# Later loads spread over ten tiles, the next pair's preparation over four, its signs a tile later

## The chip, the cores and the metric

The kernel runs on one core of one Trainium2 chip. The metric is the device time of one execution in microseconds (us); for the kernel before and after it is the median of several runs. A core has TensorE (PE in the rows, its weight loads PEld), VectorE (DVE), ScalarE (ACT), GpSimd (POOL), SyncE (SP, which here only issues DMAs) and 16 DMA engines.

## The reference

Three stages follow one another, for 2 batches of 768 rows and a width of 512.

```python
# 1: attention in hash buckets, 8 heads of 64
q_bits = (einsum('bhsd,dk->bhsk', q, proj) > 0)      # 6 bits, the same for k
mask = q_bucket[:, :, :, None] == k_bucket[:, :, None, :]
scores = np.where(mask, scale * q @ k.T, -1e9)
attn_out = softmax(scores) @ v
# 2: mixing over the rows (rank 32) and an MLP of 2048
u = x + (x.T @ U @ V).T
x = u + np.maximum(u @ w_ch1, 0.0) @ w_ch2
# 3: four causal attention experts of width 64, the two best by a gate
out = sum over e of mask_e * w_e * (softmax(causal(scale * (x wq[e]) (x wk[e]).T)) @ (x wv[e]) @ wo[e])
```

## The kernel before

The scheduler of the language puts each engine's instructions in order at build time: every instruction has a priority, its place in the program (some places are shifted), and each engine's list is filled by priority as instructions become ready in a modelled time. What the program order says is therefore not always the order on an engine; SP's queue runs in the order so found, and a DMA that waits holds all behind it.

The first attention works in pairs of heads, 4 pairs in each of 2 batches. A pair has 12 tiles of 128 query rows, 6 for each head (`a1_head`). A tile has the score matmuls (L606 with AQ and AK, L611 with BQ and BK, into PSUM tile sc), DVE's minimum on the way out (L617), ACT's exponential (L526) and then one of two ways. In most tiles P is split into a high and a low half (L528 and L534) and a DMA transposes both (L628, PT<-HL), after which 18 matmuls (L538 to L540) give po. In half of the first batch's tiles the transpose is done by TensorE in float32 (L581) with 6 matmuls L590 of four passes each.

AQ, AK, BQ and BK hold the queries and keys of a pair, split into high and low float16 parts, with the hash bits as extra rows. They are made one pair ahead: `a1_stream` calls `ahead()` when a pair begins, which calls `a1_prep` for the next pair and `a1_load` for the one after it. `a1_prep` does the following at once, in program order: ACT and DVE make QN from qn (L403, L404), a DMA transposes it to AQ (L407); ACT and POOL make KN (L408, L409), transposed to AK (L412); POOL makes the low keys KL (L414), transposed to KT (L418); plain copies bring AQ into BQ (L419) and KT into BK (L421); `a1_values` makes V (L454 POOL, L455 ACT, L456 POOL). Then `signs()`, put off by `later(wait, signs)`, computes the hash bits on TensorE (L436), compares on DVE (SG, L441) and brings them into rows of BQ and BK by four copies (L446, L447). AQ, AK, BQ, BK and V have two buffers each, qn, kn, vn, QN, KN and KL one.

`later(n, fn)` runs fn after n more tiles, and `tick()` is called once a tile; entries due at the same tick run in the order in which they were put in. The wait of the signs is SIGN_LAG (L1124), 6. The loads of a pair (`a1_load`, six of 192 KB, in the order q, k, q, k, v, v) are put off by 1 to 6 tiles (L382 to L384). When the last pair is reached, `moe2_weights` runs SIGN_LAG + 1 tiles later and loads the weights of stage 3. For the very first pair `ahead` itself is put off by two tiles.

Beside the tiles run the MLP's weight loads (`w64_unit`, 32 of 512 KB, L278, which DVE, ACT and POOL turn into float16 halves, L189 to L195 and L281 to L283), one unit for each two tiles of the first batch. The mixing of a finished pair (`x_stage_a`, `b`, `c`) follows 1, 5 and 8 tiles into the next pair. From the second batch's third pair on, TensorE also gets the MLP's matmuls (L734, L754), merged in a fixed proportion.

Of the kernel before, what the change touches and what calls it, by code (L numbers as in the profile page):

```python
# [15 lines left out]
AF = mybir.ActivationFunctionType  # L16
ALU = mybir.AluOpType
# [5 lines left out]
def kernel(  # L23
# [17 lines left out]
    nc = tc.nc  # L41
    B, H, S, D = q.shape
# [30 lines left out]
    XP = (0, 40)  # L73
    XV = True
    LUV = 4
    PLAG = (0,150)
    VLAG = 150
    PJ = nc.vector
# [34 lines left out]
    def halves(n):  # L113
        return [(c, min(512, n - c)) for c in range(0, n, 512)]
# [16 lines left out]
        out=penU, in_=penU, pattern=[[1, P]], base=0, channel_multiplier=-1,  # L131
# [11 lines left out]
    for c, kinds in enumerate(((0, 0, 1, 1), (0, 1, 0, 1))):  # L143
        for i, kind in enumerate(kinds):
# [3 lines left out]
                out=thr[sl, c : c + 1], in_=thr[sl, c : c + 1], pattern=[[0, 1]],  # L148
# [196 lines left out]
    def later(n, fn):  # L345
        pending.append([n, fn])
# [10 lines left out]
    def sooner(n, fn):  # L357
        tc.cur_priority -= n
        fn()
        tc.cur_priority += n  # L360
# [7 lines left out]
    def a1_load(b, p, spread=True):  # L368
        h0 = 2 * p
        qn = sp.tile([P, 2 * NT, D], F32, tag="qn", name=f"qn_{b}_{p}")  # L370
        kn = sp.tile([P, 2 * NT, D], F32, tag="kn", name=f"kn_{b}_{p}")
        vn = sp.tile([P, 2 * NT, D], F32, tag="vn", name=f"vn_{b}_{p}")
        jt = [slice(NT * j, NT * (j + 1)) for j in range(2)]
        todo = []
        for j in range(2):
            todo.append((qn[:, jt[j], :], q[b, h0 + j].rearrange("(t p) d -> p t d", t=NT)))
            todo.append((kn[:, jt[j], :], k[b, h0 + j].rearrange("(p t) d -> p t d", t=NT)))
        for j in range(2):
            todo.append((vn[:, jt[j], :], v[b, h0 + j].rearrange("(p t) d -> p t d", t=NT)))
        nats[b, p] = (qn, kn, vn)  # L380
        todo = [lambda d=d, s_=s_: nc.sync.dma_start(d, s_) for d, s_ in todo]
        if spread:  # L382
            for i, fn in enumerate(todo):
                later(1 + i, fn)  # L384
        return todo

    preps = {}

    def a1_prep(b, p, wait):
        qn, kn, vn = nats.pop((b, p))  # L390
        n = f"{b}_{p}"
        QN = sp.tile([P, 2 * NT, P], FH, tag="QN", name=f"QN_{n}")
        KN = sp.tile([P, 2 * NT, P], FH, tag="KN", name=f"KN_{n}")
        KL = sp.tile([P, NT, P], FH, tag="KL", name=f"KL_{n}")
        AQ = sp.tile([P, 2, NT, P], FH, tag="AQ", bufs=2, name=f"AQ_{n}")
        AK = sp.tile([P, 2, NT, P], FH, tag="AK", bufs=2, name=f"AK_{n}")
        BQ = sp.tile([P, 2, NT, P], FH, tag="BQ", bufs=2, name=f"BQ_{n}")
        BK = sp.tile([P, 2, NT, P], FH, tag="BK", bufs=2, name=f"BK_{n}")
        KT = sp.tile([P, NT, P], FH, tag="KS", bufs=2, name=f"KT_{n}")
        V = sp.tile([P, 2, 2 * NT, D], FH, tag="V", bufs=2, name=f"V_{n}")  # L400
        flat = lambda ap: ap.rearrange("p j t s -> p (j t) s")
        jt = [slice(NT * j, NT * (j + 1)) for j in range(2)]
        nc.scalar.activation(QN[:, :, 0:D], qn, AF.Copy, scale=-0.125)  # L403
        nc.vector.scalar_tensor_tensor(  # L404
            QN[:, :, D : 2 * D], QN[:, :, 0:D], 8.0, qn, op0=ALU.mult, op1=ALU.add
        )
        nc.sync.dma_start_transpose(out=flat(AQ), in_=QN)  # L407
        nc.scalar.activation(KN[:, :, 0:D], kn, AF.Copy)  # L408
        nc.gpsimd.tensor_scalar(  # L409
            KN[:, :, D : 2 * D], KN[:, :, 0:D], -0.125, 1.0, op0=ALU.mult, op1=ALU.mult  # L410
        )
        nc.sync.dma_start_transpose(out=flat(AK), in_=KN)  # L412
        for j in range(2):
            nc.gpsimd.tensor_tensor(  # L414
                KL[:, :, D * j : D * (j + 1)], kn[:, jt[j], :], KN[:, jt[j], 0:D],
                op=ALU.subtract,
            )
        nc.sync.dma_start_transpose(out=KT, in_=KL)  # L418
        nc.sync.dma_start(BQ[0:D], AQ[0:D])  # L419
        for j in range(2):  # L420
            nc.sync.dma_start(BK[0:D, j], KT[D * j : D * (j + 1)])  # L421
        preps[b, p] = (AQ, AK, BQ, BK, V)
        a1_values(b, p, vn, V)

        def signs():
            sg = psc.tile([P, 1024], F32, tag="sc", name=f"sg_{n}")
            f2 = lambda ap: ap.rearrange("p t s -> p (t s)")
            for c0, cn in halves(S):
                cs = slice(c0, c0 + cn)

                for last, ops in enumerate((
                    ((PQ, AQ[:, 0]), (PQ, AQ[:, 1]), (PK, AK[:, 0]), (PK, AK[:, 1])),
                    ((PL, AQ[:, 0]), (PL, AQ[:, 1]), (PB[:, 0], KT), (PB[:, 1], KT)),
                )):
                    for i, (w, x) in enumerate(ops):
                        nc.tensor.matmul(  # L436
                            sg[32 * i : 32 * (i + 1), cs], w, f2(x)[:, cs],
                            start=(last == 0), stop=(last == 1), skip_group_check=True,
                        )
            SG = sp.tile([P, NT, P], FH, tag="KS", bufs=2, name=f"SG_{n}")  # L440
            nc.vector.tensor_scalar(  # L441
                f2(SG), sg[:, 0:S], thr[:, 0:1], far[:, 0:1], op0=ALU.is_lt, op1=ALU.mult
            )
            rows = slice(D, D + NR)
            for j in range(2):
                nc.sync.dma_start(BQ[rows, j], SG[32 * j : 32 * j + NR])  # L446
                nc.sync.dma_start(BK[rows, j], SG[64 + 32 * j : 64 + 32 * j + NR])  # L447

        later(wait, signs)

    def a1_values(b, p, vn, V):
        f32 = any(x[0] == "F" for x in A1_MODES[b][p])
        V32 = VF[p % 2] if f32 else vn
        nc.gpsimd.tensor_scalar(V32, vn, 16.0, 1.0, op0=ALU.mult, op1=ALU.mult)  # L454
        nc.scalar.activation(V[:, 0], V32, AF.Copy)  # L455
        nc.gpsimd.tensor_tensor(V[:, 1], V32, V[:, 0], op=ALU.subtract)  # L456


    def a1_first(b, p):
        n = f"{b}_{p}"  # L460
        todo = a1_load(b, p, False)
        qn, kn, vn = nats.pop((b, p))
        QN = sp.tile([P, 2 * NT, P], FH, tag="QN", name=f"QN_{n}")
# [72 lines left out]
    def pv(o, PT, nk, vh, vl):  # L536
        for t in range(nk):
            nc.tensor.matmul(o, PT[:, t, :], vh(t), start=(t == 0), stop=False)  # L538
            nc.tensor.matmul(o, PT[:, t, :], vl(t), start=False, stop=False)  # L539
            nc.tensor.matmul(o, PT[:, nk + t, :], vh(t), start=False, stop=(t == nk - 1))  # L540
# [54 lines left out]
    def a1_head(b, p, j, xn):  # L595
# [7 lines left out]
        for t in range(NT):  # L603
# [17 lines left out]
            if mode[0] == "F":  # L621
# [6 lines left out]
            nc.sync.dma_start_transpose(out=PT, in_=HL.rearrange("p a s -> p (a s)"))  # L628
            sooner(-PLAG[b], lambda: pv(
                po[:, t, :], PT, NT,  # L630
# [59 lines left out]
    def a1_stream():  # L690
        pairs = [(b, p) for b in range(B) for p in range(NP)]
        for i, (b, p) in enumerate(pairs):
            if p == 0:
                if b == 1:
                    more_buffers(False)
            def ahead(i=i):
                if i + 1 < len(pairs):
                    a1_prep(*pairs[i + 1], SIGN_LAG)
                    if i + 2 < len(pairs):
                        a1_load(*pairs[i + 2])  # L700
                    else:
                        later(SIGN_LAG + 1, moe2_weights)

            if i == 0:
                later(2, ahead)
                later(LUV, load_uv)
            else:
                ahead()
            xn = sp.tile([P, NT, P], F32, tag="xn", bufs=XNB, name=f"xn_{b}_{p}")
            for j in range(2):  # L710
                for c in a1_head(b, p, j, xn):
                    tick()
                    yield c
            later(LAGX, lambda b=b, p=p, xn=xn: sooner(XP[p == NP - 1], lambda: x_stage_a(b, p, xn)))
# [362 lines left out]
    for fn in a1_load(0, 1, False):  # L1077
        fn()
# [42 lines left out]

    B0, B1 = BLOCKS
    a1 = a1_stream()
    SIGN_LAG = 6  # L1124
    PH1 = 56
    NA1 = B * NP * 2 * NT
    mlp = chain(*[mlp_stream(b, *blk) for b in range(B) for blk in BLOCKS[b]])
# [77 lines left out]
```

## Time and profile before

| | |
|---|---|
| median of 3 runs | 636.65 us (636.04 to 637.46) |
| profiled execution | 635.59 us, its span 633.8 us |
| PE busy | 579.1 us (91% of the span) |
| DVE busy | 422.7 us (67%) |
| ACT busy | 348.5 us (55%) |
| POOL busy | 232.1 us (37%) |
| mean granted clock of TensorE | 0.956 |
| DMA moved | 84.36 MB, mean 133 GB/s |

The shares are means over stages with different limits. In the page's picture of the span in 40 slices the DMA engines are busy for 90% and more of most of the first 14 slices and TensorE of nearly all of the last 24. A DMA share is the mean busy share of 16 DMA engines, made of the times of their packets, which can overlap, so it can stand a little above 1. A granted clock of 1.00 is TensorE at 2.4 GHz, 0.5 is 1.2 GHz; numbers between are means over a stretch. An instruction that only issues a DMA stands with the time that issuing took, not with the transfer's.

### The profile page before, as it was taken

How to read it: one execution, taken by the hardware profiler on the slowest of the kernel's cores; microseconds unless marked ns; L12 is line 12 of the kernel's file. 1: busy time of each engine (PE TensorE's matmuls, PEld its weight loads, DVE VectorE, ACT ScalarE, POOL GpSimd, SP SyncE). 2: the span in 40 equal slices, each digit the busy share in tenths (PEclk: the TensorE clock that was granted, in tenths of full speed). 3: DMA queues.
4: the chain of work that ended last, by engine and by line, in shares of the span. 5: the costliest groups of instructions: out<-in, count | busy, mean ns of one | idle time of the engine just before them, and what ended most of it. 6: DMA issues, size and time to landing. Idle time of an engine off the chain costs nothing.

```text
span 633.8 us, 16209 instructions
## 1 busy us (share of the span) xinstructions
PE 579.1 (91%) x6498; PEld 477.0 (75%) x6498; DVE 422.7 (67%) x1029; ACT 348.5 (55%) x744; POOL 232.1 (37%) x218
## 2 busy tenths in 40 slices
PE   5698888978798799989999999999999999998995
PEld 3376866757577589875888898878887888997963
DVE  6989696988877863674876555583784435465295
ACT  4769485775786652673776543462453413344273
POOL 4738777686897662231432101020040000002021
PEclk9679797889889999999999999999999999999998
DMA  8799999999989999597587602242263102016064
GB/s 234 140 218 215 243 211 244 227 228 269 219 182 251 231 178 172 101 200 114 108 130 121 101 20 50 38 84 72 46 114 67 34 15 39 27 35 109 23 107 109
DMA packets 228029, 84.36 MB, mean 133 GB/s; under 512 B 207057, under 2 KB 223473, under 8 KB 227953
## 3 DMA queue, kind: packets, MB, share of 16 engines
q1 hardware_dynamic: 227952, 83.32, 65.4%
q8 instruction: 51, 0.84, 0.6%
q14 instruction: 26, 0.20, 0.1%
HBM read 29.11 MB, written 3.15 MB: 51 GB/s over the span
## 4 chain that ended last, share of the span: by engine, by line
PE 59%; DMA 14%; DVE 7%; POOL 7%; ACT 6%; issue 5%; SPq 1%; POOLq 0%; DVEq 0%; ACTq 0%
PE px L754 18%; PE ph L734 12%; DMA PT<-HL 8%; PE po L590 3%; POOL HL L534 3%; PE pq L805 3%; PE s L908 2%; PE pk L805 2%; PE pz L1040 2%; PE pv L837 2%; ACT HL L528 2%; DVE P L617 2%; ACT P L526 2%; DMA more_hT<-more_W 2%; DMA more_hT<-HL 2%
## 5 line engine op out<-in xcount | busy, mean ns | idle before, releaser
L534 POOL TENSOR_TENSOR HL<-P,HL 128x768 f16<-128x768 f32 (+5 forms) x62 | 88.7, 1432 | 323.2 <-DVE HL L530 148.7
L734 PE MATMUL ph<-U,W 128*128 128x256 f16 (+1 forms) x1344 | 145.1, 258 | 1.7 <-DVE hT L736 1.1
L754 PE MATMUL px<-hT,W 128*128 128x256 f16 (+1 forms) x1344 | 146.1, 258 | 0.1
L734 PEld LDWEIGHTS <-W 128*128 128x128 f16 x1344 | 114.2, 98 | 17.1 <-issue 2.4
L754 PEld LDWEIGHTS <-W 128*128 128x128 f16 x1344 | 115.0, 98 | 14.3 <-issue 2.0
L526 ACT ACTIVATE P<-P,m 128x768 f32<-128x768 f32 (+5 forms) x109 | 88.7, 814 | 56.0 <-DVE P L916 28.7
L617 DVE TENSOR_SCALAR_CACHE_REDUCE P<-sc 128x768 f32<-128x768 f32 x76 | 71.9, 950 | 12.8 <-PE sc L611 8.4
L736 DVE SCALAR_TENSOR_TENSOR hT<-ph,hT 128x256 f16<-128x256 f32 (+1 forms) x112 | 42.6, 382 | 45.6 <-ACT hT L735 44.9
L528 ACT ACTIVATE HL<-P 128x768 f16<-128x768 f32 (+5 forms) x80 | 60.5, 758 | 17.6 <-DMA PT<-HL 14.8
L735 ACT ACTIVATE hT<-ph 128x256 f16<-128x256 f32 (+1 forms) x112 | 38.7, 347 | 51.3 <-PE ph L734 47.8
L538 PEld LDWEIGHTS <-PT 128*128 128x128 f16 x516 | 47.8, 99 | 23.8 <-DMA PT<-HL 20.1
L606 PE MATMUL sc<-AK,AQ 128*128 128x512 f16 x192 | 50.0, 341 | 9.3 <-DVE P L617 6.5
L538 PE MATMUL po<-V,PT 128*128 128x64 f16 x372 | 45.7, 195 | 11.5 <-DMA PT<-HL 10.6
L611 PE MATMUL sc<-BK,BQ 88*128 88x512 f16 x192 | 49.9, 340 | 0.0
L539 PEld LDWEIGHTS <-PT 128*128 128x128 f16 x516 | 47.5, 99 | 1.5 <-issue 0.2
L540 PEld LDWEIGHTS <-PT 128*128 128x128 f16 x516 | 47.4, 99 | 0.4
L540 PE MATMUL po<-V,PT 128*128 128x64 f16 x372 | 45.7, 195 | 0.0
L539 PE MATMUL po<-V,PT 128*128 128x64 f16 x372 | 45.2, 195 | 0.0
L534 DVE TENSOR_TENSOR HL<-P,HL 128x768 f16<-128x768 f32 (+5 forms) x42 | 32.3, 769 | 15.4 <-ACT HL L528 14.8
L916 DVE TENSOR_SCALAR_CACHE_REDUCE P<-s 128x128 f32<-128x128 f32 (+5 forms) x48 | 29.5, 618 | 10.9 <-PE s L913 10.6
L606 PEld LDWEIGHTS <-AQ 128*128 128x128 f16 x192 | 18.0, 105 | 17.8 <-issue 13.2
L611 PEld LDWEIGHTS <-BQ 88*128 88x128 f16 x192 | 19.5, 102 | 13.9 <-issue 2.1
(240 smaller groups left out, 1186.7 us busy)
## 6 DMA issues: line engine op xcount, KB each, us to landing
w<-in_moe_w_ch_dram SPq DMA_DIRECT2D x16, 512.0 KB
wx<-in_moe_w_ch_dram SPq DMA_DIRECT2D x16, 512.0 KB
qn<-in_q_dram SPq DMA_DIRECT2D x16, 192.0 KB
kn<-in_k_dram SPq DMA_DIRECT2D x16, 192.0 KB
vn<-in_v_dram SPq DMA_DIRECT2D x16, 192.0 KB
out_dram<-o SPq DMA_DIRECT2D x12, 256.0 KB
PT<-HL SPq DMA_TRANSPOSE x101
BQ<-AQ SPq DMA_DIRECT2D x7, 192.0 KB
```

Source lines behind the costliest of these rows:

```text
L526: nc.scalar.activation(P32, P32, AF.Exp, bias=m, scale=-1.0, accum_out=ssum)
L528: nc.scalar.activation(HL[:, 0], P32, AF.Copy)
L534: eng.tensor_tensor(HL[:, 1], P32, HL[:, 0], op=ALU.subtract)
L538: nc.tensor.matmul(o, PT[:, t, :], vh(t), start=(t == 0), stop=False)
L539: nc.tensor.matmul(o, PT[:, t, :], vl(t), start=False, stop=False)
L540: nc.tensor.matmul(o, PT[:, nk + t, :], vh(t), start=False, stop=(t == nk - 1))
L606: nc.tensor.matmul(ps[:, c0 : c0 + cn], aq[:, t, :], ak[:, c0 : c0 + cn], start=True, stop=False,)
L611: nc.tensor.matmul(ps[:, c0 : c0 + cn], bq[:, t, :], bk[:, c0 : c0 + cn], start=False, stop=True,)
L617: nc.vector.tensor_scalar(P32, ps[:, 0:S], CLIP, None, op0=ALU.min, op1=ALU.min, accum_out=m)
L734: nc.tensor.matmul(ph, w, u, start=(i == 0), stop=(i == len(ops) - 1))
L736: nc.vector.scalar_tensor_tensor(hT[1][:, ft, :], ph, 0.0, hT[0][:, ft, :], op0=ALU.max, op1=ALU.subtract)
L754: nc.tensor.matmul(po, w, u, start=(i == 0), stop=(i == len(ops) - 1))
```

## The change

The six loads of `a1_load` are due 1, 3, 5, 7, 9 and 10 tiles later instead of 1 to 6, in the order q, q, k, k, v, v. Of `a1_prep` only the allocation of the tiles, QN and the transpose to AQ stay where they were. KN and the transpose to AK come one tile later, KL, the transpose to KT and the copies into BQ and BK three, V four. The signs come 7 tiles later instead of 6, and with SIGN_LAG the weights of stage 3 one tile later.

```diff
+    PREP = (1,3,4)
+
+    LOADS = (1,3,5,7,9,10)
...
         if spread:
-            for i, fn in enumerate(todo):
-                later(1 + i, fn)
+            for i, n in zip((0, 2, 1, 3, 4, 5), LOADS):
+                later(n, todo[i])
         return todo
...
         nc.sync.dma_start_transpose(out=flat(AQ), in_=QN)
-        nc.scalar.activation(KN[:, :, 0:D], kn, AF.Copy)
-        nc.gpsimd.tensor_scalar(
-            KN[:, :, D : 2 * D], KN[:, :, 0:D], -0.125, 1.0, op0=ALU.mult, op1=ALU.mult
-        )
-        nc.sync.dma_start_transpose(out=flat(AK), in_=KN)
-        for j in range(2):
-            nc.gpsimd.tensor_tensor(
-                KL[:, :, D * j : D * (j + 1)], kn[:, jt[j], :], KN[:, jt[j], 0:D],
-                op=ALU.subtract,
-            )
-        nc.sync.dma_start_transpose(out=KT, in_=KL)
-        nc.sync.dma_start(BQ[0:D], AQ[0:D])
-        for j in range(2):
-            nc.sync.dma_start(BK[0:D, j], KT[D * j : D * (j + 1)])
         preps[b, p] = (AQ, AK, BQ, BK, V)
-        a1_values(b, p, vn, V)
+
+        def keys():
+            nc.scalar.activation(KN[:, :, 0:D], kn, AF.Copy)
+            nc.gpsimd.tensor_scalar(
+                KN[:, :, D : 2 * D], KN[:, :, 0:D], -0.125, 1.0, op0=ALU.mult, op1=ALU.mult
+            )
+            nc.sync.dma_start_transpose(out=flat(AK), in_=KN)
+
+        def keys_low():
+            for j in range(2):
+                nc.gpsimd.tensor_tensor(
+                    KL[:, :, D * j : D * (j + 1)], kn[:, jt[j], :], KN[:, jt[j], 0:D],
+                    op=ALU.subtract,
+                )
+            nc.sync.dma_start_transpose(out=KT, in_=KL)
+            nc.sync.dma_start(BQ[0:D], AQ[0:D])
+            for j in range(2):
+                nc.sync.dma_start(BK[0:D, j], KT[D * j : D * (j + 1)])
+
+        later(PREP[0], keys)
+        later(PREP[1], keys_low)
+        later(PREP[2], lambda: a1_values(b, p, vn, V))
...
-    SIGN_LAG = 6
+    SIGN_LAG = 7
```

## Rows read from the trace of the kernel before

**Rows 1.** Table of stretches: us, busy time of each engine, PEclk, DMA share, GB/s.
```profile
40.00:48.00 8.00, 8.00 (x107) 7.05 (x105) 7.83 (x16) 6.48 (x12) 1.96 (x2) 1.00 0.90 203
48.00:152.00 104.00, 89.60 (x900) 73.34 (x897) 85.53 (x166) 72.11 (x135) 78.14 (x70) 0.89 1.08 233
152.00:176.00 24.00, 18.23 (x158) 12.77 (x156) 20.74 (x40) 19.63 (x35) 21.04 (x18) 0.85 1.15 228
176.00:192.00 16.00, 15.51 (x213) 12.84 (x210) 11.78 (x24) 12.75 (x24) 15.02 (x13) 0.90 0.84 188
...
66.00:78.00 12.00, 11.60 (x127) 11.13 (x127) 6.60 (x13) 5.33 (x9) 8.10 (x8) 0.72 1.07 243
...
102.00:114.00 12.00, 11.12 (x90) 10.12 (x91) 5.60 (x11) 5.50 (x11) 6.42 (x7) 0.58 1.12 268
...
136.00:152.00 16.00, 13.28 (x140) 12.25 (x141) 11.13 (x20) 6.81 (x14) 10.74 (x11) 0.79 1.09 257
...
232.00:360.00 128.00, 123.73 (x1518) 102.46 (x1516) 81.64 (x152) 76.23 (x142) 36.93 (x27) 1.00 0.79 137
```

**Rows 2.** DVE in order of time: first tile, eighth, ninth, and the next pair's first.
```profile
50.81 0.94 DVE L617 TENSOR_SCALAR_CACHE_REDUCE P<-sc 128x768 f32<-128x768 f32 x1
...
65.51 0.94 DVE L617 TENSOR_SCALAR_CACHE_REDUCE P<-sc 128x768 f32<-128x768 f32 x1
...
77.77 0.95 DVE L617 TENSOR_SCALAR_CACHE_REDUCE more_W<-sc 128x768 f32<-128x768 f32 x1
...
84.86 0.95 DVE L617 TENSOR_SCALAR_CACHE_REDUCE P<-sc 128x768 f32<-128x768 f32 x1
```

**Rows 3.** TensorE in order of time; in brackets the wait before and what ended it.
```profile
66.40 0.24 PE L538 MATMUL po<-V,PT 128*128 128x64 f16 x1 [0.81 <-DMA PT<-more_W]
...
67.36 2.80 PE L590 MATMUL po<-more_hT,PT 128*128 128x64 f32 x12
...
73.38 1.53 PE L590 MATMUL po<-more_hT,more_hT 128*128 128x64 f32 x12
```

**Rows 4.** SP's queue in order of time: start, issuing time, line, out<-in.
```profile
45.66 0.71 SPq L447 DMA_DIRECT2D BK<-SG  x1
...
50.27 1.45 SPq L407 DMA_TRANSPOSE AQ<-QN  x1
...
56.36 1.67 SPq L418 DMA_TRANSPOSE KT<-KL  x1
...
60.99 1.45 SPq L421 DMA_DIRECT2D BK<-KT  x2
62.55 1.50 SPq L628 DMA_TRANSPOSE PT<-more_W  x1
64.10 0.87 SPq L381 DMA_DIRECT2D qn<-in_q_dram  x1
...
73.77 0.43 SPq L381 DMA_DIRECT2D vn<-in_v_dram  x1
...
74.77 0.82 SPq L446 DMA_DIRECT2D BQ<-SG  x1
...
77.21 0.71 SPq L447 DMA_DIRECT2D BK<-SG  x1
```

**Rows 5.** DMA issues by line: count and KB of each.
```profile
qn<-in_q_dram SPq DMA_DIRECT2D x16, 192.0 KB
```

**Rows 6.** ACT in order of time.
```profile
73.66 0.84 ACT L403 ACTIVATE QN<-qn 128x768 f16<-128x768 f32 x1 [0.41 <-DMA qn<-in_q_dram]
```

**Rows 7.** POOL in order of time.
```profile
75.33 0.83 POOL L409 TENSOR_SCALAR KN<-KN 128x768 f16<-128x768 f16 x1 [3.74 <-ACT KN L408]
76.12 2.50 POOL L414 TENSOR_TENSOR KL<-kn,KN 128x384 f16<-128x384 f32 x2
...
100.91 1.64 POOL L456 TENSOR_TENSOR V<-more_hT,V 128x768 f16<-128x768 f32 x1
```

**Rows 8.** The first user of stage 3's weights: first and last start.
```profile
L805 PE MATMUL pq<-U,wq x168: 217/273/273, 367.0 to 612.5; 128*128 128x256 f16 x120, 128*128 128x128 f16 x48
```

More of the change, by code (lines that the diff above doesn't have):

```diff
@@ L407, in a1_prep @@
         nc.sync.dma_start_transpose(out=flat(AQ), in_=QN)
-        nc.scalar.activation(KN[:, :, 0:D], kn, AF.Copy)
-        nc.gpsimd.tensor_scalar(
-            KN[:, :, D : 2 * D], KN[:, :, 0:D], -0.125, 1.0, op0=ALU.mult, op1=ALU.mult
-        )
-        nc.sync.dma_start_transpose(out=flat(AK), in_=KN)
-        for j in range(2):
-            nc.gpsimd.tensor_tensor(
-                KL[:, :, D * j : D * (j + 1)], kn[:, jt[j], :], KN[:, jt[j], 0:D],
-                op=ALU.subtract,
-            )
-        nc.sync.dma_start_transpose(out=KT, in_=KL)
-        nc.sync.dma_start(BQ[0:D], AQ[0:D])
-        for j in range(2):
-            nc.sync.dma_start(BK[0:D, j], KT[D * j : D * (j + 1)])
-        preps[b, p] = (AQ, AK, BQ, BK, V)
-        a1_values(b, p, vn, V)
+        preps[b, p] = (AQ, AK, BQ, BK, V)
+        def keys():
+            nc.scalar.activation(KN[:, :, 0:D], kn, AF.Copy)
+            nc.gpsimd.tensor_scalar(
+                KN[:, :, D : 2 * D], KN[:, :, 0:D], -0.125, 1.0, op0=ALU.mult, op1=ALU.mult
+            )
+            nc.sync.dma_start_transpose(out=flat(AK), in_=KN)
[12 more added lines that the diff above has]
+        later(PREP[2], lambda: a1_values(b, p, vn, V))
         def signs():
```

## The prediction

> **What bounds the kernel now.** I read the page first, for how the busy shares change along the span, then a table of stretches, then the DMA queue's and three engines' instructions in order of time around one stall. The table of stretches [rows 1] shows two kernels in one. From 48 to 152 us the DMA engines are full (share 1.08, 233 GB/s), TensorE is busy for 89.6 of 104 us, and its granted clock averages 0.89. From 152 to 176 us the share is 1.15; only 40 to 48 us (0.90) and 176 to 192 us (0.84) leave the DMA engines any air. From 232 to 360 us it is the other way round: share 0.79, TensorE busy 123.7 of 128 us at clock 1.00. The change moves only preparations and loads of the first attention, and most of those run in the first part. So the question is what the first 232 us can win while the DMA engines are full.
>
> The first part is not smooth. DVE's rows [rows 2] count the tiles: L617 is run once for each, 12 to a pair. The second pair's first tile starts at 50.81, its eighth at 65.51, its ninth only at 77.77, and the third pair's first (the 25th in all) at 84.86: a mean pitch of (84.86 - 50.81) / 12 = 2.84 us with one hole of 12.3 us. Two more such holes lie at 102 to 114 us (clock 0.58) and in 136 to 152 us (0.79) [rows 1]. In the first one the DMA share is 1.07 and TensorE is busy 11.6 of 12 us, but at a mean clock of 0.72 [rows 1]. TensorE's rows [rows 3] show how it begins: at 66.40 TensorE waits 0.81 us for the transpose PT, and the clock has fallen by then: the twelve L590 matmuls take 2.80 us at 67.36 and 1.53 us at 73.38, the 1.2 and the 2.4 GHz level.
>
> SP's queue [rows 4] shows why PT is late. It runs in order: AQ at 50.27, KT at 56.36, then BK copies at 60.99 that wait for KT to land, then PT at 62.55. The loads of the pair after next (six, of 192 KB each [rows 5]) begin at 64.10, and five of them, to 73.77, stand ahead of the four sign copies (74.77 to 77.92).
>
> **The change part by part.** Nothing is added to or taken from any engine: 7 preparations, the same DMAs, bytes and instructions. The direct sum is 0, and all depends on order.
>
> Loads. Before, six are due after tiles 1 to 6; now tiles 1, 3, 5, 7, 9, 10, in the order q, q, k, k, v, v. Up to tile 7 four are due instead of six, so by the ninth tile's due time two loads fewer are ahead in the queue: 2 x 196.6 KB / 243 GB/s (the hole's rate [rows 1]) = 1.6 us. Over five such places (three holes before 152 us, two pairs after) that is 8 us off the waits for PT. The next pair's q copy began 0.41 us after its wait, at 73.66 [rows 6], 9.6 us after the first q load's issue at 64.10 [rows 4]; the last k load, now due at tile 7, has until tile 13, 6 x 2.84 = 17 us. Loading later costs nothing as long as that holds; without it each pair would pay the missing part.
>
> Keys. ACT's copy, POOL's scaling and the AK transpose move by one tile. POOL's KN (0.83 us) waited 3.74 us at the head of POOL's queue for ACT's copy [rows 7]; with the k loads long landed that wait should shorten, but the hole hides it today, so it counts from 0 to 3.7 us a pair, and I take 0: the engine behind it is not the one that ends the hole.
>
> Low keys and KT. POOL's two subtractions (2.50 us together [rows 7]) and the KT transpose move by three tiles, with the BQ copy and the two BK copies behind it on SP. Today KT is issued at 56.36, two tiles after the pair's start, because AQ and other transposes go first [rows 4]. Three tiles after the start is 50.81 + 8.5 = 59.3, so the move is 3 us at the least and 8.5 us at the most. What is queued behind a waiting KT or BK on SP is every later PT, and TensorE waits for those. That is the main cost, from 0 (hidden) to the price of the third rival; I take 0, since the sign copies are issued by 77.92 and the next pair starts at 84.86: 7 us of cover.
>
> Values. POOL's L456 (1.64 us [rows 7]) with L454 and ACT's L455 move by four tiles, past SP and POOL instructions of those tiles. They are used by the next pair's first PV, eight tiles later. Nothing is charged; without cover it would be one 1.64 us wait a pair.
>
> Signs. One tile later, 2.84 us, with their four copies; but only three loads now stand ahead of them instead of five, 1.6 us back. Net 1.2 us out of 7 us of cover. The least cover is at the first pair: last copy issued at 45.66 [rows 4], second pair at 50.81; 5.1 us less the copy's own time. Hidden, narrowly.
>
> The weight loads of stage 3 go one tile later; their first user starts at 367.0 us [rows 8], far away. Hidden.
>
> What is kept of the 8 us? Two bounds from the stretches [rows 1]. TensorE's side: the clock lost 0.11 x 104 + 0.15 x 24 + 0.10 x 16 = 16.6 us of full speed between 48 and 192 us; no more than that can come back through shorter holes. The DMA side: in full stretches bytes taken from one wait go into a later one, and free time is 0.10 x 8 + 0.16 x 16 = 3.4 us. Since the share is over 1 in the two longest of these stretches, I take a value near the DMA end: 3.0 us. The profiled execution took 635.6 us (span 633.8 and 1.8 around it); less 3.0 that is 632.6. The median of the runs is 1.1 us above that execution, so the forecast is 633.6 us.
>
> **The rivals.** First: nothing moves, about 636.5 us. The DMA engines carry the same bytes and are full in the hole as outside it (1.07 and 1.08 [rows 1]); a PT that lands sooner in tile 8 is paid for in tiles 9 to 12, where the late k and v loads now stand. For it: all shares over 1. Against: the two stretches under 1, and the half-rate clock. The Trainium skill, "DMA: Bandwidth & Descriptors", section "Queues, rings and completion order", says that each DMA engine consumes its descriptors in ring order. By that rule alone the spread only swaps places in a full ring, which is this rival's 636.5; the trace agrees in that PT's users wait behind loads issued earlier.
>
> Second: a bigger gain, about 627 us. If the PTs come soon enough that TensorE has no such gap before the holes, the clock stays at 2.4 GHz and more than half of the 16.6 us returns: 636.65 - 9.6. For it: the hole's clock of 0.72. Against: the full DMA.
>
> Third, slower, about 642 us: the key chain becomes the bound. It decides when KT comes the whole 8.5 us later, that is when SP keeps today's lag behind the tiles. Then the sign copies begin when KT's signs are done and end at 77.92 + 8.5 = 86.4, 1.5 us after the next pair's first tile at 84.86, and each of the six later pairs starts up to 1.5 us late; I take 0.9 us of it, since a late start also lets the full ring drain, so 6 x 0.9 = 5.4 us, 642 us; with the landing of a copy behind a full ring (KT's own took up to 60.99 - 56.36 = 4.6 us) some pairs pay more. For it: signs' cover shrinks from six tiles after low keys to four. Against: SP's lag is made by the three transposes in a row, which the change takes apart.
>
> **How the numbers follow.** About 0.2% (1.3 us) is what a measurement of this kernel can tell from no change. Forecast (631 to 635.3 us) 0.38, bigger gain 0.14, nothing 0.18, slower 0.30. Faster is 0.52, same 0.18, slower 0.30. The forecast's own range is 631 to 635.3; to hold 8 in 10 it must take in most of the bigger gain and the slower case with its landing: 627 to 643 us.
>
> **What would show it.** Right: the hole between a pair's eighth and ninth tile shrinks from 12.3 us by 1.6 us or more, the mean clock from 48 to 192 us rises above 0.89, and the stretch 232 to 360 us begins with more TensorE work done. Rival one: holes move to another tile, clock and span as they were. Rival three: the first tile of a pair waits for the sign copies, or signs for KT. Wrong altogether: if the order of the whole queue comes out different, for instance if SP's order of PTs and weight loads changes far from the moved steps.

## The result, and the profile after

The kernel became slower: 641.3 us (median of 20 runs, 637.5 to 648.1) against 635.6 us for the kernel before in the same set (median of 20, 628.1 to 640.0); ratio 1.0098, 95% interval 1.0072 to 1.0124. The profiled execution took 637.5 us (span 635.8), the shortest of the 20, so the rows that follow show less than the whole loss: 2.0 us of span, where the medians show 5.7.

Table of stretches of the changed kernel, columns as in [rows 1]:

```profile
48.00:152.00 104.00, 87.35 (x899) 67.14 (x898) 88.86 (x170) 74.85 (x139) 81.15 (x71) 0.92 1.05 228
102.00:114.00 12.00, 10.05 (x128) 8.03 (x124) 10.49 (x18) 6.42 (x12) 7.63 (x7) 1.00 1.05 256
136.00:152.00 16.00, 13.35 (x132) 10.73 (x132) 10.83 (x19) 6.71 (x13) 8.10 (x8) 0.80 1.00 237
152.00:176.00 24.00, 20.10 (x206) 15.13 (x205) 19.57 (x41) 18.84 (x35) 20.57 (x18) 0.85 1.03 228
176.00:192.00 16.00, 12.42 (x144) 8.44 (x144) 10.43 (x19) 10.88 (x20) 12.56 (x10) 0.89 1.00 178
...
232.00:360.00 128.00, 124.19 (x1476) 99.82 (x1474) 79.21 (x150) 74.82 (x138) 36.70 (x27) 0.99 0.74 133
```

From 48 to 152 us the clock rose from 0.89 to 0.92 and the DMA share stayed above 1. From 232 to 360 us TensorE was busier (124.19 against 123.73 us) with fewer matmuls on record (1476 against 1518): that stretch got dearer.

DVE of the changed kernel in order of time, the answer to [rows 2] (second pair's first, eighth and ninth tile, third pair's first):

```profile
52.98 0.95 DVE L627 TENSOR_SCALAR_CACHE_REDUCE P<-sc 128x768 f32<-128x768 f32 x1
...
68.64 0.96 DVE L627 TENSOR_SCALAR_CACHE_REDUCE P<-sc 128x768 f32<-128x768 f32 x1 [1.12 <-PE sc L621]
76.01 0.96 DVE L627 TENSOR_SCALAR_CACHE_REDUCE more_W<-sc 128x768 f32<-128x768 f32 x1
...
83.42 0.95 DVE L627 TENSOR_SCALAR_CACHE_REDUCE P<-sc 128x768 f32<-128x768 f32 x1
```

The hole is 7.4 us instead of 12.3 and the third pair starts at 83.42 instead of 84.86. The 49th tile starts at 156.6 instead of 160.9, the 61st at 194.9 instead of 199.0. Yet the 96th, the last, starts at 354.6 instead of 352.0, and what follows it is 281 us long in one and 282 in the other. So in this execution 4.1 us were won up to the 61st tile and 6.7 lost between it and the last.

SP's queue of the changed kernel around the same pair, the answer to [rows 4]:

```profile
63.41 1.85 SPq L426 DMA_TRANSPOSE KT<-KL  x1
...
68.75 1.18 SPq L429 DMA_DIRECT2D BK<-KT  x2
...
76.22 0.82 SPq L456 DMA_DIRECT2D BQ<-SG  x1
...
78.65 0.71 SPq L457 DMA_DIRECT2D BK<-SG  x1
```

KT is issued 7.1 us later than before, the last sign copy 1.4 us later, 4 us ahead of the next pair's first tile.

TensorE of the changed kernel, a piece of the 7th pair's signs:

```profile
250.63 0.49 PE L744 MATMUL ph<-U,W 128*128 128x256 f16 x3
251.05 0.39 PE L446 MATMUL sg<-AK,PK 128*32 128x512 f16 x1
251.37 0.28 PE L744 MATMUL ph<-U,W 128*128 128x256 f16 x1
251.59 0.39 PE L446 MATMUL sg<-AK,PK 128*32 128x512 f16 x1
251.91 0.28 PE L744 MATMUL ph<-U,W 128*128 128x256 f16 x1
252.12 0.39 PE L446 MATMUL sg<-AQ,PL 128*32 128x512 f16 x1
```

TensorE of the kernel before, the last ten of the same 16 matmuls:

```profile
222.29 0.39 PE L436 MATMUL sg<-KT,PB 128*32 128x512 f16 x2
222.30 0.29 PE L436 MATMUL sg<-AQ,PQ 128*32 128x256 f16 x2
222.41 0.28 PE L436 MATMUL sg<-AQ,PL 128*32 128x256 f16 x2
222.52 0.28 PE L436 MATMUL sg<-AK,PK 128*32 128x256 f16 x2
222.62 0.28 PE L436 MATMUL sg<-KT,PB 128*32 128x256 f16 x2
222.83 0.50 PE L734 MATMUL ph<-U,W 128*128 128x256 f16 x3
```

Read starts, not durations (those overlap). Before, ten sign matmuls take 0.54 us: each uses 32 of the array's 128 columns (a column group), and neighbours of other column groups run side by side. In the changed kernel sign and MLP matmuls alternate: a sign takes 0.32 us to the next start, and the MLP matmul behind it 0.22 us, where the 135 in a row from 225.33 us in the kernel before take 14.90 us, 0.11 each. 14 of the 7th pair's 16 signs moved from ahead of the MLP's px block (192 matmuls L754, begun at 225.3 us) to behind it. The 8th pair's signs alternate in both kernels, 3.88 us in 14 runs before and 3.33 us in 11 after.

### The profile page after: what moved, and what is told of

Its sections match the earlier page's. It is cut to its first block, busy times and chain, and to the rows that moved or that the text cites. A ratio compares the mean times of both kernels' runs of the same rounds, so it can differ in the third digit from the quotient of the medians.

```text
span 635.8 us, 16211 instructions
## 1 busy us (share of the span) xinstructions
PE 579.7 (91%) x6498; PEld 471.4 (74%) x6498; DVE 422.2 (66%) x1029; ACT 349.1 (55%) x744; POOL 233.4 (37%) x218
## 4 chain that ended last, share of the span: by engine, by line
PE 59%; DMA 19%; POOL 7%; DVE 6%; issue 4%; ACT 3%; SPq 2%; DVEq 0%; POOLq 0%; ACTq 0%
PE px L764 17%; PE ph L744 14%; DMA PT<-HL 13%; PE pq L815 3%; PE s L918 2%; POOL HL L544 2%; PE pk L815 2%; PE pz L1050 2%; PE po L600 2%; DMA more_hT<-more_W 2%; PE pv L847 2%; PE sc L616 2%; PE sc L621 2%; PE po L548 1%; PE sg L446 1%
## 5 line engine op out<-in xcount | busy, mean ns | idle before, releaser
L744 PE MATMUL ph<-U,W 128*128 128x256 f16 (+1 forms) x1344 | 147.0, 260 | 1.3 <-ACT U L212 0.7
L745 ACT ACTIVATE hT<-ph 128x256 f16<-128x256 f32 (+1 forms) x112 | 38.8, 347 | 54.7 <-PE ph L744 52.5
L616 PE MATMUL sc<-AK,AQ 128*128 128x512 f16 x192 | 52.8, 358 | 11.8 <-DVE P L627 8.3
L548 PE MATMUL po<-V,PT 128*128 128x64 f16 x372 | 45.1, 196 | 14.7 <-DMA PT<-HL 12.6
L621 PE MATMUL sc<-BK,BQ 88*128 88x512 f16 x192 | 53.6, 361 | 0.0
L550 PE MATMUL po<-V,PT 128*128 128x64 f16 x372 | 45.1, 195 | 0.0
L549 PE MATMUL po<-V,PT 128*128 128x64 f16 x372 | 44.8, 195 | 0.0
L616 PEld LDWEIGHTS <-AQ 128*128 128x128 f16 x192 | 19.4, 109 | 21.9 <-issue 16.7
```

Of the source, the lines that this page charges most:

```text
L616: nc.tensor.matmul(ps[:, c0 : c0 + cn], aq[:, t, :], ak[:, c0 : c0 + cn], start=True, stop=False,)
L621: nc.tensor.matmul(ps[:, c0 : c0 + cn], bq[:, t, :], bk[:, c0 : c0 + cn], start=False, stop=True,)
L744: nc.tensor.matmul(ph, w, u, start=(i == 0), stop=(i == len(ops) - 1))
```

## The experiments

The pairs count from 1 here; where an expectation says pair 5, 6 or 7, it counts from 0. All times stand beside the kernel before on the same chip.

**Which part?** Theory K: the keys' chain comes late, as in the third rival. L: the late loads. M: no part alone. First the loads alone:

```diff
-            for i, fn in enumerate(todo):
-                later(1 + i, fn)
+            for i, n in zip((0, 2, 1, 3, 4, 5), (1, 3, 5, 7, 9, 10)):
+                later(n, todo[i])
```

> Only the loads change (1, 3, 5, 7, 9, 10 tiles, in the order q, q, k, k, v, v); preparation at once and signs after 6 tiles as before. Theory K (the key chain: KT three tiles later and the signs behind it make the loss of 1.0%): ratio to before 0.995 to 1.002. Theory L (the loads, single and late, cost it by standing between the transposes): ratio 1.007 to 1.012. Theory M (no part alone, the sum of the order does): within 0.3% of 1.

Measured: 639.6 us against 635.5, 1.0070 (1.0047 to 1.0093). Then the preparation alone, apart over 1, 3 and 4 tiles as in the change, with the old loads and lag:

> Only the preparation is taken apart over 1, 3 and 4 tiles; loads and signs (6 tiles) as before. Theory K: ratio 1.006 to 1.012. Theory L: within 0.3% of 1. Theory M: within 0.3% of 1.

Measured: 642.2 us, 1.0113 (1.0074 to 1.0153). The lag alone:

```diff
-    SIGN_LAG = 6
+    SIGN_LAG = 7
```

> Only the signs (and stage 3's weight loads) come one tile later; loads and preparation as before. Theory K: ratio 1.000 to 1.004, since KT is early and only 2.84 us of the cover go. Theory L and M: within 0.3% of 1.

Measured: 643.8 us, 1.0150 (1.0115 to 1.0185). Loads and preparation, lag 6:

> Loads and preparation as in the changed kernel, but signs after 6 tiles. Theory K: ratio 1.004 to 1.012, less of it than in the changed kernel if the signs' tile matters. Theory L: ratio 1.007 to 1.012. Theory M: below 1.005.

Measured: 641.7 us, 1.0116 (1.0075 to 1.0157). Each part alone costs about as much as the whole (4.1, 6.7 and 8.3 us against 5.7), and they don't add. That fits none of K, L and M, and points to something that any of the parts disturbs. In all four traces the 7th pair's signs end behind the px block, among other matmuls (255.7 to 263.0 us), as in the changed kernel.

**Signs in a block, for all pairs.** Theory P: the lost side-by-side running costs the time. H: the signs' PSUM tile holds a score slot across the px block. N: neither.

```diff
-        later(wait, signs)
+        later(wait, lambda: sooner(150, signs))
```

In the changed kernel:

> The changed kernel with one thing more: a pair's 16 sign matmuls are put ahead of the MLP's work by 150 priority steps, so that they stand in one block on TensorE instead of one to one with the MLP's matmuls (for the 7th pair in 3 runs instead of 12 or so, for the 8th in one). Nothing else of the change is undone: loads, preparation and lag stay. In the traces of the kernel before, the 7th pair's 16 sign matmuls cost 1.48 us in two runs, while in the changed kernel and in all four partial versions they stand between the MLP's matmuls and cost 3.0 to 4.0 us, in a stretch in which TensorE has no free time. Theory P (what was lost is the side-by-side running of the sign matmuls, four in a row on four column groups): 3 to 5 us less than the changed kernel, 636 to 638 against 641, the pair-6 and pair-7 signs below 2 us each. Theory H (the signs' tile holds one of the two score slots from the first sign matmul to the last, across the px block of 192 MLP matmuls): the first signs still come before that block and the last behind it (234 matmuls between), so at most 1 us less, 640 to 641. Theory N (neither; the loss is in the order of the DMAs): the same as the changed kernel within 1 us.

Measured: 644.8 us against 636.5, 1.0131 (1.0087 to 1.0174). In the kernel before:

> The kernel before, whole, with only the sign matmuls put ahead of the MLP's work by 150 priority steps. It moves the 7th pair's signs to the place they have in the changed kernel, behind the px block of 192 MLP matmuls (position 1910 of TensorE's order instead of ahead of 1680), but in one block; and the 8th pair's signs become one block, which before cost 3.88 us in 14 runs. Theory P: the place is harmless and the packing counts: 7th pair's signs 1 to 1.5 us as before, 8th pair's 2 to 2.5 us less, so 633 against 635.5 (ratio 0.996). Theory H or another in which the place before the px block counts (one tile of the pair fewer ahead of that block): 2 to 4 us slower than before, 638 to 640. Theory N: the same as before.

Measured: 640.6 us, 1.0073 (1.0040 to 1.0106). With the change's loads and lag and the low keys one tile late:

> The change with its loads over ten tiles and its lag of 7, the keys' low halves one tile after the queries instead of three (values still four tiles later), and the signs put ahead by 150. Its 7th pair's signs stand ahead of the px block (positions 1662 to 1689, px from 1690) in two runs, and the 8th pair's in one. It gives both theories what they want: theory P expects packed signs in both pairs, theory H a score slot that isn't held across the px block. Both: the gain of the first half kept, 631 to 634 against 635.5 before. Theory N: 640 to 642, like the parts alone.

Measured: 640.9 us, 1.0079 (1.0047 to 1.0111). With the loads alone:

> The loads part alone (ten tiles, preparation at once, lag 6), which ran at 639.6 us, with the signs put ahead by 150 priority steps: the 7th pair's signs come ahead of the px block (positions 1628 to 1671, px from 1672, 3 runs) and the 8th pair's in one block. Theory P: 3.0 us of sign matmuls become 1.5 at the 7th pair and 3.9 become 1.5 at the 8th, so 3 to 4 us less than that part alone, 635 to 636.5. Theory H: the 8th tile of pair 5 is again early (230 instead of 259 us) and 3 us come back, 636 to 637. Theory N: 639 to 640. P and H aren't told apart by this run; it shows whether the loads part itself loses anything once TensorE's order is put right.

Measured: 643.8 us, 1.0131 (1.0081 to 1.0182). P missed all four times. H missed too, but for e6, where its 638 to 640 was nearly met; N's forecast came true in the third run alone. In the traces the signs behind 240 us did run in rows, and cheaply (0.76 us for 16 at e6's 8th pair). In three of the four the time was lost ahead of that: their px blocks ended at 258.7, 252.1 and 254.4 us, against 243.7 in the changed kernel and 244.0 in the loads part. In e6 the block ended 1.0 us later than in the kernel before and the time was lost behind it, with three more tiles left to do and TensorE idle for 9.2 us up to the 96th tile instead of 4.1. The last of the MLP's 32 weight loads, issued at 211.4 us in the kernel before and 214.4 in the changed one, came at 229.1, 223.2, 219.1 and 224.0 us. Putting every pair's signs ahead had changed the order of the whole queue. So the next edit touched the last pairs only.

**Signs in a block, for the last pairs alone.** Theory F: up to some 220 us the DMA queue bounds, behind that TensorE, and there alternating signs cost 3 us a pair. G: the signs don't matter. In the changed kernel:

```diff
-        later(wait, signs)
+        later(wait, (lambda: sooner(150, signs)) if (b, p) >= (1, 2) else signs)
```

> The changed kernel, with the sign matmuls of the 7th and 8th pair alone put ahead of the MLP's work by 150 priority steps; TensorE's order and the DMA queue's are those of the changed kernel up to some 215 us. In place of 12 and 11 runs among the MLP's matmuls the two pairs' signs then stand in 2 runs and 1. Theory F (the first 240 us are bound by the full DMA queue, which is why putting all signs ahead lost 3 to 5 us there; behind them TensorE is bound and 16 sign matmuls cost 0.8 us side by side and 3.6 us one to one with others): both pairs save 2.5 to 3 us and nothing is lost ahead of them, 636 us against 641, about the time of the kernel before. Theory G (the loss behind 240 us lies in the tile that comes late, not in the signs): at most 1 us less than the changed kernel, 640 to 641.

Measured: 636.7 us against 635.5, 1.0013 (0.9981 to 1.0045): 4.5 us under the changed kernel. Its first signs of the 7th pair start at 223.6 us and its last at 248.6, so they hold the PSUM tile across the px block as well: H falls, since the time came back all the same. In the kernel before, with `(b, p) == (1, 3)`, which leaves every order up to 285 us as it was:

> The kernel before with the sign matmuls of the 8th pair alone put ahead of the MLP's work, so that they stand in one run and not in 14; everything up to some 290 us keeps its order on every engine. Theory F: 3.88 us of sign matmuls become 0.8 in a stretch where TensorE is busy for 47.7 of 50 us, so 2.5 to 3 us less than the kernel before, 632.5 to 633 against 635.5 (ratio 0.996). Theory G: no change, within 0.5 us.

Measured: 632.5 us, 0.9944 (0.9903 to 0.9985), faster than both kernels. TensorE of this one at the 8th pair's signs:

```profile
286.15 0.39 PE L446 MATMUL sg<-AQ,PQ 128*32 128x512 f16 x2
286.15 0.39 PE L446 MATMUL sg<-AK,PK 128*32 128x512 f16 x2
286.37 0.38 PE L446 MATMUL sg<-AQ,PL 128*32 128x512 f16 x2
286.38 0.38 PE L446 MATMUL sg<-KT,PB 128*32 128x512 f16 x2
286.59 0.28 PE L446 MATMUL sg<-AQ,PQ 128*32 128x256 f16 x2
...
286.91 0.48 PE L677 MATMUL tp<-xs,UU 128*96 128x128 f16 x5
```

16 signs from 286.15 to 286.91: 0.76 us in place of 3.88, and the 13 MLP matmuls that stood between them pay 0.11 us less each, 1.4 us: 4.5 us of TensorE's time, of which the median shows 3.0. (In the profiled execution TensorE waited 0.7 us longer behind the px block and had half the clock from 290.0 to 293.4 us.) With the loads part (600 in place of 150):

> The loads part alone (ten tiles, preparation at once, lag 6; it ran at 639.6 us) with the sign matmuls of the 7th and 8th pair put ahead by 600 priority steps: 3 runs instead of 12, beginning ahead of the px block, and 1 instead of 14. Its first 200 us are those of the loads part. Theory F: 2 to 2.5 us back at the 7th pair and 3 at the 8th, 634 to 635 us, at or a little under the kernel before; against the kernel before with only its last pair put right (632.5 to 633) the loads part then gains nothing. Theory G: 639 to 640.

Measured: 634.6 us, 0.9984 (0.9955 to 1.0013), 5 us under the loads part as it was. G falls in all three. The one miss among these four was the attempt to price the side-by-side running by itself, with the sign loop turned so that the four matmuls of a column group follow each other:

```diff
-            for c0, cn in halves(S):
...
-                    for i, (w, x) in enumerate(ops):
+            for i in range(4):
+                for c0, cn in halves(S):
...
+                    for last, (w, x) in enumerate((high[i], low[i])):
```

> The kernel before with the 16 sign matmuls of every pair written column group by column group, so that almost none can run beside the one ahead of it; the same instructions, and the same place of each pair's block on TensorE. It prices the side-by-side running by itself and asks at once which parts TensorE bounds: a block in a row at 2.4 GHz then costs 8 times 0.21 and 8 times 0.11 us, 2.6 us in place of 0.8, so 1.8 us a pair. Theory F: the 7th pair loses 1.8 us, the 8th, which stands among other matmuls already, nothing, and the first five pairs (in the part that the DMA queue bounds) nothing or little: 637 to 638 us. If TensorE bounds the first part as well, all six pairs pay, half of them at half the clock: 646 us or more. Theory G: 635.5, no change.

Measured: 636.0 us, 1.0002 (0.9975 to 1.0028), no change. Its TensorE shows that the edit did not undo what it should:

```profile
134.60 0.40 PE L444 MATMUL sg<-AQ,PQ 128*32 128x512 f16 x2
134.63 0.40 PE L444 MATMUL sg<-AK,PK 128*32 128x512 f16 x2
134.83 0.39 PE L444 MATMUL sg<-AQ,PL 128*32 128x512 f16 x2
134.85 0.39 PE L444 MATMUL sg<-KT,PB 128*32 128x512 f16 x2
```

The matmuls of all four groups start together though they were queued group by group; 16 take 0.80 us against 0.77. That they were queued so shows at the 8th pair, where each sign stands alone among MLP matmuls: AQ,PQ at 292.28, AQ,PL at 292.82, AQ,PQ at 293.35, AQ,PL at 293.78 us, then the next group. Nothing follows on the price; it stays with the rows above and with e7, e8 and e10.

**What is left, and what bounds the first part.** With the signs put right in both, the changed kernel (636.7) is still 4.2 us behind the kernel before (632.5). F2: every part keeps a loss of its own ahead of 222 us. G2: nothing is left but the loads' part. The preparation with the last two pairs' signs ahead by 150:

> The preparation part alone (keys, low keys and values one, three and four tiles later; loads and lag as before; it ran at 642.2 us) with the 7th and 8th pair's sign matmuls put ahead of the MLP's work by 150 priority steps, 2 runs and 1. With the signs put right in both, the whole change stands at 636.7 us and the kernel before at 632.5: 4.2 us are left, of which the loads part alone has 2.1 (634.6). Theory F2 (what is left is the rate at which the DMA engines are fed before 222 us, when the in-order queue holds transposes that wait): this part takes the signs' 5 us off 642.2 and keeps a loss, 636.5 to 637.5, and fewer bytes moved by 222 us than the 40.2 MB of the best one, about 39.2. Theory G2 (nothing is left beside the signs, the 4.2 us are the loads' alone): 632.5 to 633.

Measured: 638.2 us against 636.0, 1.0056 (1.0027 to 1.0085). The lag alone with the last two pairs' signs ahead by 600:

> The lag of 7 alone (loads and preparation as before; it ran at 643.8 us), with the sign matmuls of the last two pairs put ahead by 600 priority steps: 3 runs from 34 matmuls behind the px block's start, and 1. Theory F2: 2.5 to 3 us back for each of the two pairs, and the loss ahead of 222 us stays (1.7 MB fewer moved by then in the part alone, at 229 GB/s 7 us, of which the medians showed half): 637 to 639 us. Theory G2: 632.5 to 633.

Measured: 636.2 us, 1.0033 (0.9997 to 1.0068). Both parts got 4 to 8 us back and both stay above 632.5, so G2 falls; F2's times were missed by under 1 us (638.2 over its 637.5, 636.2 under its 637). Its other sign came: of the bytes, the DMA engines moved 39.2 MB from 48 to 222 us in e11, as forecast, where the kernel before moved 39.9 and e8 40.2. The table below has this for every run. Then the kernel before with half of the weights' bytes; it leaves out the other half and uses the loaded half twice:

```diff
-        nc.sync.dma_start(o, src)
-        from_f64(w, st, name)
+        if len(src.shape) == 3:
+            nc.sync.dma_start(o[:, 0:2], src[:, 0:2])
+        else:
+            nc.sync.dma_start(o[:, 0:512], src[:, 0:512])
+        half = st[:, 0:256].unsqueeze(1).to_broadcast([P, 2, 256, 2])
+        from_f64(w.rearrange("p (h a) -> p h a", h=2), half, name)
```

> The kernel before with half of each MLP weight tile loaded (256 KB instead of 512 KB a load) and used twice, so it leaves out half the weights: 7.3 MB of the 43.3 MB between 48 and 240 us fall away, and the tiles, matmuls and vector work stay. The order of the queue differs in places. Theory F (the DMA queue bounds the first 222 us): 7.3 MB at 229 GB/s are 32 us, and at least a third of that comes back before TensorE or a tile's chain bounds: 610 to 625 us. If a tile's own chain of engines bounds there: 632 to 636 us, and the DMA share of 48 to 152 us falls below 0.9 at an unchanged pitch of the tiles.

Measured: 626.6 us against 636.0, 0.9885 (0.9830 to 0.9941), 9.4 us less and 1.6 us short of what F gave. Its stretches:

```profile
48.00:152.00 104.00, 90.00 (x901) 71.43 (x900) 90.18 (x175) 78.55 (x146) 82.81 (x73) 0.88 0.99 203
152.00:222.00 70.00, 63.64 (x766) 51.76 (x766) 60.85 (x113) 53.50 (x101) 61.42 (x51) 0.94 1.07 204
```

The bytes fall from 233 to 203 GB/s and the share only from 1.08 to 0.99: packets under 512 bytes fill most of it (0.65 of the 1.08 before by their times, 0.69 of the 0.99 here), the weights are the smaller part. The 49th tile starts at 152.3 us instead of 160.9 at the same clock (0.88 against 0.89), the px block at 213.8 instead of 225.3. The order of the queue differs a little too, but no order with all of the weights brought these two points before 156.6 and 221.5 us. So the DMA engines bound the first part, though less than a third of the bytes' 32 us came back; what takes over before that, a tile's own chain or the small packets, isn't shown.

**Two halves of the span.** The last px matmul of the first block parts the traces well: up to it the queue's load counts, behind it TensorE's. From SP's, TensorE's and DVE's rows in order of time (starts in us; the last column is the 96th tile less the last px):

| kernel | MB moved, 48 to 222 us | last weight load | last px of the block | 96th tile | behind the block |
|---|---|---|---|---|---|
| before | 39.9 | 211.4 | 246.2 | 352.0 | 105.8 |
| changed | 39.6 | 214.4 | 243.7 | 354.6 | 110.9 |
| e1 (loads) | 39.7 | 215.5 | 244.0 | 356.9 | 113.0 |
| e2 (preparation) | 38.8 | 217.4 | 248.6 | 360.3 | 111.6 |
| e3 (lag) | 38.2 | 218.9 | 248.5 | 361.1 | 112.6 |
| e4 (loads, preparation) | 38.9 | 219.3 | 249.8 | 358.4 | 108.6 |
| e5, e6 (all pairs' signs) | 37.3, 38.5 | 229.1, 223.2 | 258.7, 247.2 | 365.2, 360.3 | 106.5, 113.1 |
| low keys one tile late, loads part (all pairs' signs) | 38.6, 38.4 | 219.1, 224.0 | 252.1, 254.4 | 360.0, 362.6 | 107.8, 108.1 |
| e7 (changed, signs in rows) | 39.2 | 218.5 | 247.8 | 353.4 | 105.6 |
| e8 (before, signs in rows) | 40.2 | 210.5 | 245.4 | 349.0 | 103.6 |
| e9 (before, signs by group) | 39.9 | 211.5 | 246.6 | 353.4 | 106.8 |
| e10 (loads, signs in rows) | 39.7 | 214.2 | 243.6 | 351.9 | 108.3 |
| e11 (preparation, signs in rows) | 39.2 | 215.4 | 247.7 | 355.8 | 108.1 |
| e12 (lag, signs in rows) | 37.8 | 219.9 | 249.4 | 357.6 | 108.2 |

The old order (before, e8, e9) moved 39.9 to 40.2 MB and ended the block at 245.4 to 246.6 us. The preparation alone and the lag alone moved 0.7 to 2.1 MB less than the kernel before, in both of their executions, and ended it 1 to 4 us later. The loads alone ended it some 2 us earlier, with about the bytes of the old order, and lose behind it: there TensorE waited 8.2 us for transposed tiles (PT) in e10, against 4.8 in e8.

## Why the prediction was wrong

**What bounds the kernel: right.** The DMA engines bound the first part (e13), TensorE the second (e7, e8).

**Loads and holes: the sign came, but not by the loads.** Two executions each show the old order (the kernel before and e8, alike on SP up to 285 us) and the changed one (the changed kernel and e7, alike up to 245 us). The hole is 12.3 and 12.7 us in the old order and 7.4 in both of the changed one. But the loads alone leave it at 11.0 (e1) and 12.6 us (e10): the 1.6 us that two loads fewer were to take off it are not there. The preparation alone, with the old loads, has 5.6 us at this tile in e2 and e11, and 8.1 and 6.8 two tiles earlier, so part of the hole only moved. DVE in order of time, the second pair's eighth and ninth tile in e10, then its sixth to ninth in e2:

```profile
65.32 0.94 DVE L627 TENSOR_SCALAR_CACHE_REDUCE P<-sc 128x768 f32<-128x768 f32 x1
77.92 0.95 DVE L627 TENSOR_SCALAR_CACHE_REDUCE more_W<-sc 128x768 f32<-128x768 f32 x1
```
```profile
63.38 0.95 DVE L627 TENSOR_SCALAR_CACHE_REDUCE P<-sc 128x768 f32<-128x768 f32 x1
71.45 0.96 DVE L627 TENSOR_SCALAR_CACHE_REDUCE P<-sc 128x768 f32<-128x768 f32 x1 [4.90 <-PE sc L621]
73.41 0.96 DVE L627 TENSOR_SCALAR_CACHE_REDUCE P<-sc 128x768 f32<-128x768 f32 x1 [0.67 <-PE sc L621]
79.03 0.95 DVE L627 TENSOR_SCALAR_CACHE_REDUCE more_W<-sc 128x768 f32<-128x768 f32 x1
```

The other signs don't stand clear of what one order shows in two executions: the next hole is 12.9 and 10.8 us in the old order, 10.2 and 10.5 in the changed one; the clock from 48 to 192 us averages 0.881 and 0.905 against 0.905 and 0.941. The px block ended 2.5 us earlier in the changed kernel (243.7 against 246.2), where 3.0 were forecast, but at 247.8 in e7: that the size came out is luck. The forecast also added 1.1 us, from the profiled execution to the median of three runs; they weren't there in the set of 20, whose median is 635.6 as well.

**What is kept of it: wrong.** The gain of the profiled execution isn't one to count on, as e7 shows. The upper bound from the clock had no ground. Windows from 48 to 152 us, first e9, then e7, then e12:

```profile
48.00:152.00 104.00, 86.02 (x909) 67.50 (x908) 86.50 (x166) 72.41 (x136) 78.52 (x69) 0.93 1.08 232
```
```profile
48.00:152.00 104.00, 82.92 (x910) 65.19 (x906) 88.54 (x169) 75.10 (x141) 79.79 (x70) 0.97 1.06 227
```
```profile
48.00:152.00 104.00, 88.83 (x839) 73.94 (x839) 81.22 (x156) 70.31 (x131) 74.69 (x66) 0.82 1.03 221
```

Their 49th tiles start at 161.9, 160.0 and 163.8 us; the kernel before has 0.89 and 160.9 [rows 1], e10 0.87 and 159.1. The one at 0.82 is also the one that moved the fewest bytes (221 GB/s); from 0.87 to 0.97 a higher clock brings no earlier tile, and of the two executions of the changed order the one at 0.92 has the 49th tile at 156.6, the one at 0.97 at 160.0. It fits that TensorE at half rate there only fills time in which it would have waited; no run tests that by itself. And the first rival's swap did happen: by the 49th tile 24 weight loads were issued in the old order (before and e8) and 22 in the changed one (both executions). The tiles came 4 us sooner and the last weight load 3.0 us later (214.4), in e7 1 us sooner and 7 us later.

**Low keys, values, signs "hidden": wrong, and this is the step that failed.** The prediction charged 0 for the low keys and KT, the values and the signs. Its cover was counted on SP's queue, from the copies to the next pair's first tile, and there it held: 4 us were left. Yet the preparation alone cost 6.7 us (e2) and the lag alone 8.3 (e3); the loads, which were to cost nothing, cost 4.1 (e1). The prediction had asked neither where the 16 sign matmuls would stand on TensorE nor how the queue would feed the DMA engines far from the moved steps.

The signs on TensorE are the smaller part. They need AQ, AK and KT. KT was issued 7.1 us later in the first hole's pair and 8.3 in the 7th (224.86 us, 216.55 before), behind the start of the px block (222.8); in the order found at build time all but two of the 7th pair's signs fell behind that block, into a stretch without free time. The loads alone (KT at 219.5 us) and the lag alone had the same effect, on 10 and all 16 of the signs. The 14 behind the block cost 3.0 us (251.05 to 255.9 us less the matmuls between), and some 10 matmuls between them about 0.1 us more each, 1.1 us; before, the 16 cost 0.9 us beside waits for AQ and AK. That is 3.2 us more at the 7th pair and 0.9 less at the 8th: 2.3 us in the trace. The medians agree, though their intervals are as wide as this: signs in rows take 0.85% off the changed kernel (e7) and 0.56% off the kernel before (e8), and only the difference, 0.3% or some 2 us of the 5.7, can be the change's doing.

Behind the block the profile of the changed kernel loses 5.1 us (110.9 against 105.8), and the terms can be counted on TensorE. The 7th pair's signs and what stands between them are 4.1 us, none of which stood there before; the 8th pair's are 0.9 less. The score matmuls of one more tile were left, 67 tiles' against 68 being done by the block's end: 0.65 us (330.49 to 331.15 for one tile); the po matmuls left were as many. The clock was at its lower level from 278.7 to 282.1 us, behind a wait of 2.3 us for a PT in the 7th pair: up to 1.7 us more. In the kernel before, with a wait of 1.8 us at the same place, it stayed at the upper one. TensorE's waits were 0.3 us shorter. These make 5.3. e7 brought the 110.9 back to 105.6, with the same tile left over.

The rest, 4.2 us by the medians of e7 and e8 (whose intervals just touch), is not the signs'. For the preparation and the lag the table shows fewer bytes moved up to 222 us, 0.7 to 2.1 MB; at the 229 GB/s of the kernel before in that stretch a MB is 4.4 us.

**The third rival** has 642 us, near the time that came, by a mechanism that did not happen: no first tile of a pair waited for the sign copies (issued by 79.4 us, tile at 83.4). Its time is no credit to it.

**Keys: right.** The KN that waited 3.74 us on POOL [rows 7] starts at 85.00 us without a wait, and so does that of the pair ahead of it, which had waited 2.99; no gain of it shows (the preparation alone, which moves the keys, was slower):

```profile
53.12 0.83 POOL L415 TENSOR_SCALAR KN<-KN 128x768 f16<-128x768 f16 x1
```

**What would make it wrong** had been named, "if the order of the whole queue comes out different"; it should have been a rival with a price.

**Open.** Between e7 and e8 (4.2 us by the medians, 4.4 in the traces up to the 96th tile) 2.4 us lie up to the end of the px block, with the last weight load issued 8.0 us later, and 2.0 behind it: 0.65 the scores of one more tile, 0.8 the 7th pair's signs, which e8 has ahead of the block, and 0.7 more waiting. That the preparation and the lag keep a loss of their own is shown (the ratios of e11 and e12 are 1.1 and 0.9% above that of e8, clear of their intervals); for the loads (e10, 0.4%) the intervals overlap. Which place in the queue makes it is not shown, and two executions of the changed order differ by 4.1 us at the end of the block.

## What to carry to other kernels

When a step that feeds TensorE is moved, ask which instructions of a full stretch it will land among, as well as whether its result is still in time; and where one queue feeds full DMA engines, compare the bytes moved by a fixed time, not one hole. Small matmuls that run side by side belong in one block, and a block that alternates with another stream can be put right by its priority alone, for the pairs concerned (632.5 us here, better than both kernels); the same for all pairs came out 8 to 9 us slower than for the last ones (e5, e6 and the loads part against e7, e8 and e10). A low granted clock in a stretch that the DMA engines fill is a symptom, and no bound for a gain.

## What the runs showed of the hardware

Matmuls of 32 columns in different column groups overlapped even when queued group by group (16 in 0.80 us in e9, 0.77 when four of different groups follow each other). Alternating with matmuls of 128 columns costs both kinds: 0.32 us a sign of 512 and 0.22 us an MLP matmul of 256, where a row of the latter takes 0.11 each. The Trainium skill, "TensorEngine Tiling (Array Packing)", section "Key Properties", says that tiles of the array work independently, and that a change of the tiling mode, unlike a change of the tile, drains TensorE. The rows agree with both: groups overlap, and each MLP matmul pays 0.11 us more between signs. Whether a drain is what it pays, these rows can't tell.
